# Attention and mixture of experts on one core: two more sets of prepared buffers, paid for by work in place

## The chip, the cores and the metric

The kernel runs on one core of one Trainium2 chip. The metric is the device time of one execution in microseconds. The core's engines work side by side, each through its own list of instructions in order: TensorE (PE, with PEld for its weight loads), VectorE (DVE), ScalarE (ACT), GpSimd (POOL) and SyncE (SP), which here only issues DMAs. An instruction that waits holds up everything behind it on its engine.

## The reference

Four batches of eight heads, 768 tokens, head size 40, run a recurrence with a decaying state; its output, laid out as 3072 tokens of 320 features, goes through a dense mixture of eight experts whose gate is balanced in eight rounds.

```python
for t in range(S):
    y[:, :, t] = np.einsum('bhd,bhde->bhe', rt, state)
    Sa = np.einsum('bhde,bhe->bhd', state, at)
    state = state * wt[:, :, None, :] - np.einsum('bhd,bhe->bhde', Sa, bt) + np.einsum('bhd,bhe->bhde', vt, kt)
...
P = np.exp(logits - logits.max())
for _ in range(8):
    P /= P.sum(1, keepdims=True) + 1e-09
    P /= P.sum(0, keepdims=True) + 1e-09
    P *= N / E
for e in range(E):
    out += P[:, e:e + 1] * (np.maximum(x @ w1[e], 0.0) @ w2[e])
```

## The kernel before

**Two phases.** `attention` runs the recurrence in chunks of 64 tokens: 12 chunks by 4 batches make 48 blocks, numbered 4c + b here. The mixture of experts follows and is the rest of the span. Its first eight blocks, like the whole attention phase, are put in order by a planner that simulates the engines' lists while the program is built; from its ninth block on (`N_MAN = 8`) the order is the one written.

**Preparing a block** is `prep(c, b)`. SyncE loads `inp` (112 rows of decays, k, b and a). VectorE scans the decays forward (`q`, L123), takes a reciprocal, and scans backward (`gf`, L133). SyncE stores `gf` to DRAM (`gd`, L137), from where the recurrence loads it as `gr`. GpSimd scales k and b (`kb`, L147) and a (`ab`, L153 and L154; VectorE does this for the first eight blocks). TensorE multiplies them (`ll`, L159). VectorE masks one half of the product into `sx` (L169), and ScalarE copies the other half, after `sx`, to `lt` (L173) and stores it to DRAM (`ld`, L178). What the recurrence needs later (`sx`, `bb`, `cc`) stays in one of `NSX = 20` sets, taken in turn. The first preparations use the last eight sets as scratch: `IN_SETS` for the load, `KB_SETS` for `kb` and `lt`. From block 8 on, `inp` is one of two buffers in turn; `gf` has two buffers of its own, and `lt` has one.

**Inverting.** The 48 blocks form six groups of eight. When all eight `ld` blocks of a group have landed, SyncE loads them into `lu` (L367) and VectorE inverts 128 triangular 32x32 matrices at once: seven pairs of product (L184) and sum (L187), then pairs L193 and L196 for the off-diagonal parts of size 8, 8 and 16. The part of size 16 is built with 2048 products at a time in `pr`. `finish` copies the inverse transposed (L356), and SyncE stores it twice (`ud`, `nd`). `tload` and `tmat` fetch it back for the two chunks of the group as `tt`.

**The recurrence** is `recur(c, b)`, in five steps spread over time. One block takes, among others, `f` (L269), `pm` (L289, which needs `tt`) and `ws` (L296) on VectorE, six groups of matmuls on TensorE, and `y` on GpSimd.

**Order.** The calls are sorted by a due time written by hand (`ev`), and the planner then fills each engine's list from them. Loads and stores all stand in SyncE's one list, except that `ld` from block 8 on is issued by ScalarE.

Of the kernel before, what the change touches and what calls it, by code (L numbers as in the profile page):

```python
# [11 lines left out]
F32 = mybir.dt.float32  # L12
# [17 lines left out]
def attention(ctx, tc, d, xd, ps, pq, pt, gs, lg):  # L30
    nc = tc.nc
# [6 lines left out]
    dr = ctx.enter_context(tc.tile_pool(name="a_dr", bufs=2, space=bass.MemoryType.DRAM))  # L38
    dr1 = ctx.enter_context(tc.tile_pool(name="a_dr1", bufs=1, space=bass.MemoryType.DRAM))

    cst = const.tile([128, 64 + 64 + 104 + 128 + 40 + 260], F32, name="cst")
    nc.sync.dma_start(out=cst, in_=d["cst"])
    mask_u = cst[0:64, 0:64]
    mask_f = cst[0:R2, 64:128]
    mask_p = cst[:, 128:232]
    ident = cst[:, 232:360]
    one65 = cst[0:RP, 400:660]
# [26 lines left out]
    c1_b = [const.tile([R2, NP, 104], F32, name=f"c1{i}") for i in range(2)]  # L74
    unf = inv.tile([128, 1056], F32, name="un")
    luf = inv.tile([128, 1056], F32, name="lu")
    prf = inv.tile([128, 2048], F32, name="pr")
    gtf = inv.tile([128, 256], F32, name="gt")
    un, lu, tn = (t[:, 0:1024].rearrange("u (a b) -> u a b", b=32) for t in (unf, luf, prf))
    und, lud = (t.rearrange("u (b x) -> u b x", x=264)[:, :, 0:256].rearrange("u b (c j) -> u b c j", j=32)  # L80
# [19 lines left out]
    def first_use(i):  # L100
        if i in fresh:
            fresh.discard(i)
            nc.gpsimd.memset(bb_b[i], 0.0)
            nc.scalar.copy(out=sx_b[i][64:128].rearrange("r p h x -> r (p h) x")[:, :, 64:104],
                           in_=cst[64:128, 360:400].unsqueeze(1).broadcast_to([64, 8, 40]))

    state = {"sx": 0, "ab": 0, "g1": 0, "vz": 0, "c1": 0, "tt": 0, "f": 0, "rb": 0, "x1": 0}

# [7 lines left out]
    def prep(c, b, ld):  # L116
        cb = c * NB + b
        inp = raws[IN_MAP[cb]][0:RP, 0:1029] if IN_MAP.get(cb) else pin.tile([RP, 1029], F32, name="inp", bufs=2)
        nc.sync.dma_start(out=inp, in_=d["inp"][c, b])
# [3 lines left out]
        nc.vector.tensor_tensor_scan(  # L123
            out=qf.rearrange("r p t -> r (p t)"), data0=inp[:, 0:260], data1=one65,
            initial=0.0, op0=ALU.mult, op1=ALU.add)
        q = qf[0:R2]
        g1 = rot("g1", g1_b)
        nc.vector.reciprocal(out=g1[:, :, 64], in_=qf[:, :, 64])
        sx = rot("sx", sx_b)
        i = next(j for j in range(NSX) if sx_b[j] is sx)  # L130
        bb, cc = bb_b[i], cc_b[i]
        gf = pin.tile([RP, NP, 65], F32, name="gf", bufs=2)
        nc.vector.tensor_tensor_scan(  # L133
            out=gf.rearrange("r p t -> r (p t)")[:, 259::-1], data0=inp[:, 260:0:-1],
            data1=g1.rearrange("r p t -> r (p t)")[:, 259::-1], initial=0.0, op0=ALU.mult, op1=ALU.add)
# [19 lines left out]
        nc.scalar.copy(out=sx[64:128, :, 0, 0:64], in_=ab[0:64, :, 0:64])
        nc.scalar.copy(out=sx[64:128, :, 1, 0:64], in_=ab[64:128, :, 64:128])
        ll = pq.tile([128, NP, 2, 64], F32, name="ll", tag="pq")
        for p in range(NP):
            nc.tensor.matmul(ll[:, p], lhsT=kb[:, p], rhs=ab[0:kb.shape[0], p], start=True, stop=True)  # L159
# [9 lines left out]
        nc.vector.tensor_tensor(  # L169
            out=sx[0:64, :, :, 0:64], in0=ll[0:64],  # L170
            in1=mask_u.unsqueeze(1).unsqueeze(1).broadcast_to([64, NP, 2, 64]), op=ALU.mult)
        if cb >= NKB:
            nc.scalar.activation(out=lt, in_=ll[64:128], func=AF.Copy, scale=-1.0)  # L173
        nc.scalar.copy(out=sx[0:64, :, :, 64:104], in_=kt[0:64, :, :, 0:40])
        nc.scalar.activation(out=bb[0:64, :, 0:40], in_=kt[64:128, :, 0, 0:40], func=AF.Copy, scale=-1.0)
        nc.scalar.activation(out=bb[64:128, :, 64:104], in_=kt[64:128, :, 1, 0:40], func=AF.Copy, scale=-1.0)
        if cb >= NKB:
            (nc.sync if cb < N_SP else nc.scalar).dma_start(out=ld[GRP[c][1], :, b], in_=lt)  # L178
        return dict(cc=cc, sx=sx, bb=bb)
# [15 lines left out]
            in1=m.unsqueeze(1).broadcast_to([nu, n_c, n_k, n_r]), op=ALU.mult)  # L195
        nc.vector.tensor_reduce(out=dst, in_=prv.rearrange("u c k r -> u c r k"), op=ALU.add, axis=AX.X)  # L196

    def inv_off(us, o, n, h):
        gt = gtf[us, 0:n * n].rearrange("u (c r) -> u c r", r=n)
        un_, lu_ = un[us], lu[us]  # L200
        if h == n:
            contract(us, gt, un_[:, o:o + n, o:o + n], lu_[:, o:o + n, o + n:o + 2 * n])
            contract(us, un_[:, o:o + n, o + n:o + 2 * n], gt, un_[:, o + n:o + 2 * n, o + n:o + 2 * n])
            return
        contract(us, gt[:, 0:h], un_[:, o:o + h, o:o + n], lu_[:, o:o + n, o + n:o + 2 * n])
        contract(us, gt[:, h:n], un_[:, o + h:o + n, o + h:o + n], lu_[:, o + h:o + n, o + n:o + 2 * n])
        contract(us, un_[:, o:o + n, o + n:o + n + h], gt[:, :, 0:h], un_[:, o + n:o + n + h, o + n:o + n + h])
        contract(us, un_[:, o:o + n, o + n + h:o + 2 * n], gt, un_[:, o + n:o + 2 * n, o + n + h:o + 2 * n])

    INV = [(inv_diag, (i,)) for i in range(1, 8)] + [(inv_off, a) for a in ((0, 8, 8), (16, 8, 8), (0, 16, 8))]  # L210
# [172 lines left out]
    for c in range(NCH):  # L383
# [3 lines left out]
        t = 5 * c + 2 - T_LEAD  # L387
# [67 lines left out]
def body(ctx, tc, d, out):  # L455
    nc = tc.nc
# [301 lines left out]
def _layout(inputs):  # L758
# [41 lines left out]
    cst[64:128, 64:128] = 1.0  # L800
    cst[0:64, 128:192] = up
    cst[64:128, 128:192] = up
    cst[:, 192:232] = 1.0
    cst[:, 232:360] = np.eye(128)
    cst[64:104, 360:400] = np.eye(40)
    cst[:, 400::65] = 1.0
# [20 lines left out]
```

## Time and profile before

| | |
|---|---|
| median of three runs | 1840.97 us (1838.9 to 1845.11) |
| profiled execution | 1844.61 us, its span 1842.7 us |
| granted TensorE clock, mean of the span | 0.961 |
| busy: PE, DVE, ACT, POOL | 94%, 75%, 46%, 47% |
| attention, to the last recurrence step | about 517 us |
| the six inverse copies (L356) start at | 95.23, 157.35, 234.02, 308.66, 382.89, 442.69 us |

The shares of busy time are means over two phases that differ. From 517 us on, in the mixture of experts, TensorE works nearly without a break. In the attention phase no engine is full, and what counts there is which wait ends last in each stage. The copies of the six inverses cut that phase into stages.

### The profile page before, as it was taken

The page shows a single profiled execution, that of the slowest core. Times are in us where ns is not written, and L with a number is a line of the kernel's source. Part 1 is how long each engine was busy: PE and PEld are TensorE (multiplying, and loading weights), DVE is VectorE, ACT ScalarE, POOL GpSimd, SP SyncE. Part 2 cuts the span into 40 slices and gives each one's busy share as a digit, 9 for nine tenths or more (in the row PEclk, how much of TensorE's full clock was granted, in tenths as well). Part 3 has the DMA queues.
Part 4 walks back from the last instruction along what each step waited for, and adds up shares of the span by engine and source line. Part 5 has one row for each costly group of instructions (what it writes and reads, how often), then busy time and mean ns, then how long its engine had stood idle before and what let it go on. Part 6 is the DMA issues. An engine that isn't in the chain of part 4 may idle for free.

```text
span 1842.7 us, 31504 instructions
## 1 busy us (share of the span) xinstructions
PE 1732.1 (94%) x11851; PEld 1697.6 (92%) x11851; DVE 1387.3 (75%) x2319; ACT 856.0 (46%) x1848; POOL 857.4 (47%) x844
## 2 busy tenths in 40 slices
PE   5488888899989999999999999999999999999999
PEld 4378888888889999999999999999999999999999
DVE  8876968877688768677776868977686877777676
ACT  6346667665643534344343433445343443425342
POOL 6545545532662617355371826007191744628170
PEclk8579899999899999999999999999999999999999
DMA  8467887875820102011110202201020111102001
GB/s 215 128 151 165 188 182 184 183 175 130 207 74 31 57 4 71 22 53 39 37 58 17 76 19 69 65 12 57 19 75 20 56 38 38 57 19 75 6 33 43
DMA packets 194957, 145.10 MB, mean 79 GB/s; under 512 B 143861, under 2 KB 171637, under 8 KB 194805
## 3 DMA queue, kind: packets, MB, share of 16 engines
q1 hardware_dynamic: 189013, 137.09, 28.7%
q10 hardware_dynamic: 5792, 6.00, 1.2%
q8 instruction: 94, 1.54, 0.3%
q14 instruction: 58, 0.48, 0.1%
HBM read 117.00 MB, written 26.04 MB: 78 GB/s over the span
## 4 chain that ended last, share of the span: by engine, by line
PE 73%; DVE 13%; DMA 7%; issue 3%; ACT 2%; POOL 1%; SPq 1%; ACTq 0%; DVEq 0%; POOLq 0%
PE op L636 36%; PE p L571 33%; DVE pr L193 2%; DVE un L196 2%; DMA inp<-in_inp_dram 2%; DVE gt L196 1%; DVE q L123 1%; DMA ld<-lt 1%; DMA lu<-ld 1%; DVE gf L133 1%; DMA td<-nd 1%; PE pu L287 1%; PE ll L159 1%; DMA rb<-in_r_dram 1%; DVE pm L289 1%
## 5 line engine op out<-in xcount | busy, mean ns | idle before, releaser
L571 PE MATMUL p<-xch,wh 128*128 128x384 f32 (+1 forms) x1792 | 604.8, 339 | 8.9 <-DVE sm L589 5.2
L592 ACT ACTIVATE hh<-sm 128x384 fp32r<-128x384 f32 x512 | 269.5, 527 | 725.3 <-DVE sm L589 725.3
L636 PE MATMUL op<-wh,hh 128*128 128x320 f32 x1536 | 476.8, 311 | 1.0 <-ACT hh L592 0.9
L636 PE MATMUL op<-wl,hh 128*128 128x320 f32 x1536 | 474.7, 310 | 0.0
L636 PE MATMUL op<-wh,hl 128*128 128x320 f32 x1536 | 467.3, 310 | 0.8 <-DVE hl L595 0.8
L517 POOL TENSOR_TENSOR wl<-ws,wh 128x640 fp32r<-128x640 f32 x60 | 103.0, 1716 | 608.3 <-ACT wh L515 608.2
L595 DVE SCALAR_TENSOR_TENSOR hl<-sm,hh 128x384 fp32r<-128x384 f32 x512 | 371.1, 758 | 2.4 <-ACT hh L592 2.0
L571 PEld LDWEIGHTS p<-xch,wh 128*128 128x128 f32 (+1 forms) x1792 | 337.2, 188 | 12.6 <-DVE sm L589 6.3
L571 PE MATMUL p<-xcl,wh 128*128 128x384 f32 x896 | 302.5, 338 | 0.0
L571 PE MATMUL p<-xch,wl 128*128 128x384 f32 x896 | 301.7, 337 | 0.0
L636 PEld LDWEIGHTS op<-wh,hh 128*128 128x128 f32 x1536 | 290.2, 189 | 1.6 <-ACT hh L592 1.5
L636 PEld LDWEIGHTS op<-wl,hh 128*128 128x128 f32 x1536 | 291.0, 189 | 0.0
L636 PEld LDWEIGHTS op<-wh,hl 128*128 128x128 f32 x1536 | 287.2, 188 | 1.1 <-DVE hl L595 1.0
L589 DVE TENSOR_TENSOR sm<-p,u 128x384 f32<-128x384 f32 x384 | 233.1, 617 | 8.8
L589 DVE TENSOR_TENSOR sm<-p,p 128x384 f32<-128x384 f32 x128 | 71.3, 557 | 129.8 <-PE p L571 76.3
L571 PEld LDWEIGHTS p<-xcl,wh 128*128 128x128 f32 x896 | 168.7, 188 | 0.0
L571 PEld LDWEIGHTS p<-xch,wl 128*128 128x128 f32 x896 | 168.6, 188 | 0.0
L589 DVE TENSOR_TENSOR p<-p,p 128x384 f32<-128x384 f32 x128 | 71.2, 556 | 102.6 <-PE p L571 102.2
L589 DVE TENSOR_TENSOR u<-p,p 128x384 f32<-128x384 f32 x128 | 70.9, 554 | 59.4 <-PE p L571 58.2
L525 POOL TENSOR_TENSOR wl<-ss,wh 128x512 fp32r<-128x512 f32 x60 | 89.7, 1496 | 28.3 <-ACT wh L522 24.2
L300 POOL TENSOR_TENSOR y<-ws,gr 104x256 f32<-104x256 f32 x48 | 47.1, 980 | 113.1 <-DVE ws L296 99.9
L700 DVE SCALAR_TENSOR_TENSOR acc<-op,pmat,acc 128x320 f32<-128x320 f32 x168 | 91.3, 544 | 4.5 <-PE op L636 4.4
(160 smaller groups left out, 2717.4 us busy)
## 6 DMA issues: line engine op xcount, KB each, us to landing
ws<-in_wts_dram SPq DMA_DIRECT2D x60, 832.0 KB
inp<-in_inp_dram SPq DMA_DIRECT2D x42, 450.2 KB
rb<-in_r_dram SPq DMA_DIRECT2D x48, 224.0 KB
gd<-gf SPq DMA_DIRECT2D x48, 113.8 KB
gr<-gd SPq DMA_DIRECT2D x48, 113.8 KB
vz<-in_v_dram SPq DMA_DIRECT2D x48, 112.0 KB
ld<-lt ACTq DMA_DIRECT2D x40, 128.0 KB
f<-in_vt_dram SPq DMA_DIRECT2D x48, 80.0 KB
```

What stands on the lines that cost most here:

```text
L123: nc.vector.tensor_tensor_scan(out=qf.rearrange("r p t -> r (p t)"), data0=inp[:, 0:260], data1=one65, initial=0.0, op0=ALU.mult, op1=ALU.add)
L193: nc.vector.tensor_tensor(out=prv, in0=a.unsqueeze(3).broadcast_to([nu, n_c, n_k, n_r]), in1=m.unsqueeze(1).broadcast_to([nu, n_c, n_k, n_ ...
L196: nc.vector.tensor_reduce(out=dst, in_=prv.rearrange("u c k r -> u c r k"), op=ALU.add, axis=AX.X)
L300: nc.gpsimd.tensor_tensor(out=y[:, :, b % 2], in0=ws[:, :, 0:64], in1=gr[0:R2, :, 64:0:-1], op=ALU.mult)
L517: g.tensor_tensor(out=wl[:, 0:640], in0=raw[:, 256:896], in1=wh[:, 0:640], op=ALU.subtract)
L525: g.tensor_tensor(out=lv[:, 3:7], in0=so[:, :, 0], in1=hv[:, 3:7, 0], op=ALU.subtract)
L571: nc.tensor.matmul(o, lhsT=w_, rhs=x_, start=(j == 0), stop=(j == 3))
L589: eng.tensor_tensor(out=out, in0=x, in1=y, op=ALU.add)
L592: nc.scalar.activation(out=hh[:, f, h], in_=sm[f][:, h], func=AF.Relu)
L595: v.scalar_tensor_tensor(out=hl[:, f, h], in0=sm[f][:, h], scalar=0.0, in1=hh[:, f, h], op0=ALU.max, op1=ALU.subtract)
L636: nc.tensor.matmul(ops[i], lhsT=a[:, h, cs], rhs=w_[:, cw], start=(f == 0 and h == 0 and j == 0), stop=(last and h == 1 and j == 2))
L700: nc.vector.scalar_tensor_tensor(out=acc[:, m], in0=ops[i], scalar=pmat[:, n, e:e + 1], in1=acc[:, m], op0=ALU.mult, op1=ALU.add)
```

## The change

The sets of prepared buffers become 22. The room comes from four places. The backward scan writes over the decays that it reads, in the load's buffer, so that `gf` has no buffer of its own, and `gd` is stored from there. From block 8 on, `lt` is written over the part of `inp` that held k and b, and `ld` is stored from there. The product tile `pr` shrinks from 2048 to 1024 elements, and the inverse's part of size 16 is built in six pieces that leave out rows and columns known to be zero, where four stood before. The table of constants loses its repeated parts. The gate's matrix, the ones and the identity of the second phase get their buffers after the attention phase has given up its own; the other buffers of the second phase stay where they were. The warm-up before the first inverse's end has seven matmuls of 296 columns instead of four of 512.

```diff
-    cst = const.tile([128, 64 + 64 + 104 + 128 + 40 + 260], F32, name="cst")
+    cst = const.tile([128, 64 + 104 + 128 + 260], F32, name="cst")
...
-    prf = inv.tile([128, 2048], F32, name="pr")
+    prf = inv.tile([128, 1024], F32, name="pr")
...
-        gf = pin.tile([RP, NP, 65], F32, name="gf", bufs=2)
+        gf = inp[:, 1:261].rearrange("r (p t) -> r p t", p=NP)
         nc.vector.tensor_tensor_scan(
-            out=gf.rearrange("r p t -> r (p t)")[:, 259::-1], data0=inp[:, 260:0:-1],
+            out=inp[:, 260:0:-1], data0=inp[:, 260:0:-1],
             data1=g1.rearrange("r p t -> r (p t)")[:, 259::-1], initial=0.0, op0=ALU.mult, op1=ALU.add)
         gd[c, b] = dr1.tile([RP, 260], F32, name=f"gd{cb}")
-        nc.sync.dma_start(out=gd[c, b], in_=gf.rearrange("r p t -> r (p t)"))
+        nc.sync.dma_start(out=gd[c, b], in_=inp[:, 1:261])
...
             kb = kb1
-            lt = pin.tile([64, NP, 2, 64], F32, name="lt")
+            lt = inp[0:64, 261:773].rearrange("r (p k t) -> r p k t", p=NP, k=2)
...
-    def inv_off(us, o, n, h):
+    def inv_off(us, o, n, rows):
...
+        m, e = o + n, o + 2 * n
+        for a, b in rows:
+            contract(us, gt[:, a:b], un_[:, o + a:o + b, o + a:m], lu_[:, o + a:m, m:e])
+        for a, b in [(n - y, n - x) for x, y in reversed(rows)]:
+            contract(us, un_[:, o:m, m + a:m + b], gt[:, :, 0:b], un_[:, m:m + b, m + a:m + b])
+
+    INV = [...] + [(inv_off, a) for a in ((0, 8, ((0, 8),)), (16, 8, ((0, 8),)), (0, 16, ((0, 4), (4, 8), (8, 16))))]
...
-        for _ in range(4):
-            nc.tensor.matmul(fl, lhsT=unf[:, 384:512], rhs=cst[:, 0:512], start=True, stop=True)
+        for _ in range(7):
+            nc.tensor.matmul(fl[:, 0:296], lhsT=unf[:, 384:512], rhs=cst[:, 0:296], start=True, stop=True)
...
-NSX = 20
+NSX = 22
...
-IN_SEQ = (19,18,17,16,0,0,19,18)
+IN_SEQ = (21, 20, 19, 18, 0, 0, 21, 20)
...
-        nc.gpsimd.memset(ones, 1.0)
-        nc.sync.dma_start(out=ident, in_=d["cst"][:, 232:360])
+    mid = ctx.enter_context(tc.tile_pool(name="mid", bufs=1))
...
+    nc.gpsimd.memset(ones, 1.0)
+    nc.sync.dma_start(out=ident, in_=d["cst"][:, 168:296])
```

The planner makes new lists from this, and three places of them matter here.

**SyncE behind the third inverse's copy, with the waits of each DMA.** Names with DMAHW are counters of DMAs that have landed, the others counters of an engine. Before, with the loads of the next group's `lu` ahead:

```order
L367 DMA lu<-ld 16x32x32 [waits DMAHW6_49,DMAHW2_49]
L367 DMA lu<-ld 16x32x32 [waits DMAHW7_49]
L367 DMA lu<-ld 16x32x32 [waits DMAHW0_49]
L367 DMA lu<-ld 16x32x32 [waits DMAHW1_49]
L257 DMA gr<-gd_965 112x260 [waits Pool_49]
L137 DMA gd_2660<-gf 112x260 [waits DMAHW3_49,DVE_49]
L119 DMA inp<-in_inp_dram 112x1029 [waits DMAHW4_49]
L255 DMA rb_212<-in_r_dram 112x512 [waits DMAHW5_49,PE_49]
L259 DMA f_209<-in_vt_dram 64x8x40 [waits DMAHW6_49]
L119 DMA inp<-in_inp_dram 112x1029 [waits DMAHW7_49,Pool_49]
```

Now, between the fetch of the inverse (`td`, `tt`) and the loads of `lu`, which come later:

```order
L222 DMA td<-nd 32x16x32 [waits DMAHW0_49]
L119 DMA inp<-in_inp_dram 112x1029 [waits DMAHW5_49,DMAHW1_49,Activation_49]
L224 DMA td<-ud 32x16x32 [waits DMAHW2_49]
L224 DMA td<-ud 32x16x32
L228 DMA tt_210<-ud 32x16x32 [waits DMAHW4_49]
L228 DMA tt_210<-ud 32x16x32
L228 DMA tt_210<-ud 32x16x32 [waits DMAHW6_49]
L228 DMA tt_210<-ud 32x16x32 [waits DMAHW7_49]
L301 DMA xd<-y 40x4x128 [waits DMAHW1_49]
L137 DMA gd_2334<-inp 112x260 [waits DMAHW2_49,DVE_49]
L301 DMA xd<-y 40x4x128 [waits DMAHW3_49]
L119 DMA inp<-in_inp_dram 112x1029 [waits DMAHW0_49,DMAHW4_49,Activation_49,Pool_49]
```

A load of `inp` used to wait for GpSimd, the last reader of the buffer's old contents, where it waited for an engine at all. It now waits for ScalarE, which writes `lt` into the buffer, and for the store of that `lt` to have landed. The two loads in the rows of before are those of blocks 33 and 34; block 32's stood three rows above them, and block 31's ahead of the inverse's stores. Those in the rows of now are blocks 31 and 32, so that block 31, the last of the group that `lu` waits for, is only loaded behind the inverse before it.

**VectorE ahead of the fourth inverse** (its first product is the row L184; the numbers behind `sx` are those of buffers). Before:

```order
L169 TENSOR_TENSOR sx_166<-ll,cst 64x8x64
L269 TENSOR_TENSOR f_209<-av,cst 104x8x64
L296 TENSOR_TENSOR ws<-c_2579,c_221 104x416
L289 TENSOR_TENSOR pm<-pu,cst 128x416
L123 SCALAR_TENSOR_TENSOR q<-inp,cst 112x260
L128 RECIPROCAL g_215<-q 112x4
L133 SCALAR_TENSOR_TENSOR gf<-inp,g_215 112x260
L269 TENSOR_TENSOR f_210<-av,cst 104x8x64
L184 TENSOR_TENSOR pr<-un,lu 128x4
```

Now:

```order
L123 SCALAR_TENSOR_TENSOR q<-inp,cst 112x260
L327 COPY lg<-lp 128x8
L128 RECIPROCAL g_224<-q 112x4
L133 SCALAR_TENSOR_TENSOR inp<-inp,g_224 112x260
L169 TENSOR_TENSOR sx_175<-ll,cst 64x8x64
L286 TENSOR_TENSOR pm<-pu,cst 128x416
L169 TENSOR_TENSOR sx_178<-ll,cst 64x8x64
L266 TENSOR_TENSOR f_217<-av,cst 104x8x64
L184 TENSOR_TENSOR pr<-un,lu 128x4
```

The last `sx` of the inverse's own group (block 31: `sx_166` before, `sx_175` now) stood four rows ahead of the scans of block 32; it now stands behind them.

**VectorE at the end of the first inverse** (the copy L356, now L353). Before:

```order
L169 TENSOR_TENSOR st_171<-ll,cst 64x8x64
L193 TENSOR_TENSOR pr<-gt,un 128x2048
L123 SCALAR_TENSOR_TENSOR q<-inp,cst 112x260
L196 TENSOR_REDUCE un<-pr 128x16x8
L128 RECIPROCAL g_215<-q 112x4
L169 TENSOR_TENSOR st_172<-ll,cst 64x8x64
L356 COPY pr<-un 128x1024
L133 SCALAR_TENSOR_TENSOR gf<-inp,g_215 112x260
L123 SCALAR_TENSOR_TENSOR q<-inp,cst 112x260
L128 RECIPROCAL g_215<-q 112x4
L133 SCALAR_TENSOR_TENSOR gf<-inp,g_215 112x260
L184 TENSOR_TENSOR pr<-un,lu 128x4
```

Now:

```order
L193 TENSOR_TENSOR pr<-gt,un 128x768
L133 SCALAR_TENSOR_TENSOR inp<-inp,g_224 112x260
L196 TENSOR_REDUCE un<-pr 128x16x4
L193 TENSOR_TENSOR pr<-gt,un 128x1024
L196 TENSOR_REDUCE un<-pr 128x16x4
L353 COPY pr<-un 128x1024
L169 TENSOR_TENSOR sx_187<-ll,cst 64x8x64
L123 SCALAR_TENSOR_TENSOR q<-inp,cst 112x260
L128 RECIPROCAL g_224<-q 112x4
L133 SCALAR_TENSOR_TENSOR inp<-inp,g_224 112x260
L169 TENSOR_TENSOR st_190<-ll,cst 64x8x64
L123 SCALAR_TENSOR_TENSOR q<-inp,cst 112x260
```

Before, 17 of the 48 scans `q` stood ahead of this copy, and four rows, with one more scan `q`, stood between the copy and the second inverse. Now 14 stand ahead, and three more preparations follow the copy before the second inverse. Up to the second copy there are `ws` of six blocks instead of four, and up to the last copy of 38 instead of 37.

More of the change, by code (lines that the diff above doesn't have):

```diff
@@ L39, in attention @@
     dr1 = ctx.enter_context(tc.tile_pool(name="a_dr1", bufs=1, space=bass.MemoryType.DRAM))
-    cst = const.tile([128, 64 + 64 + 104 + 128 + 40 + 260], F32, name="cst")
+    cst = const.tile([128, 64 + 104 + 128 + 260], F32, name="cst")
     nc.sync.dma_start(out=cst, in_=d["cst"])
     mask_u = cst[0:64, 0:64]
[L44 to L47, printed above, removed]
+    mask_f = cst[0:R2, 0:64]
+    mask_p = cst[:, 64:168]
+    ident = cst[:, 168:296]
+    one65 = cst[0:RP, 296:556]
     NTB = 2
@@ L104, in first_use @@
             nc.scalar.copy(out=sx_b[i][64:128].rearrange("r p h x -> r (p h) x")[:, :, 64:104],
-                           in_=cst[64:128, 360:400].unsqueeze(1).broadcast_to([64, 8, 40]))
+                           in_=ident[64:128, 64:104].unsqueeze(1).broadcast_to([64, 8, 40]))
     state = {"sx": 0, "ab": 0, "g1": 0, "vz": 0, "c1": 0, "tt": 0, "f": 0, "rb": 0, "x1": 0}
@@ L196, in contract @@
         nc.vector.tensor_reduce(out=dst, in_=prv.rearrange("u c k r -> u c r k"), op=ALU.add, axis=AX.X)
-    def inv_off(us, o, n, h):
+    def inv_off(us, o, n, rows):
         gt = gtf[us, 0:n * n].rearrange("u (c r) -> u c r", r=n)
         un_, lu_ = un[us], lu[us]
[L201 to L210, printed above, removed]
+        m, e = o + n, o + 2 * n
[3 more added lines that the diff above has]
+            contract(us, un_[:, o:m, m + a:m + b], gt[:, :, 0:b], un_[:, m:m + b, m + a:m + b])
+    INV = [(inv_diag, (i,)) for i in range(1, 8)] + [(inv_off, a) for a in ((0, 8, ((0, 8),)), (16, 8, ((0, 8),)), (0, 16, ((0, 4), (4, 8), (8, 16))))]
     def tload(c):
@@ L425 @@
 KB_POOL = (1,2,3,4,5,6,7)
-IN_SETS = (19, 18, 17, 16)
-KB_SETS = (15, 14, 13, 12)
-IN_SEQ = (19,18,17,16,0,0,19,18)
+IN_SETS = (21, 20, 19, 18)
+KB_SETS = (17, 16, 15, 14)
+IN_SEQ = (21, 20, 19, 18, 0, 0, 21, 20)
 IN_MAP = dict(enumerate(IN_SEQ))
@@ L461, in body @@
     one = ctx.enter_context(tc.tile_pool(name="one", bufs=1))
-    pmat = one.tile([128, 24, E], F32, name="pmat")
     lg = one.tile([128, 24, E], F32, name="lg")
-    ones = one.tile([128, 128], F32, name="ones")
-    ident = one.tile([128, 128], F32, name="ident")
     gs = one.tile([R2, NP, E], F32, name="gs")
@@ L472, in body @@
         attention(actx, tc, d, xd, ps, pq, pt, gs, lg)
-        nc.gpsimd.memset(ones, 1.0)
-        nc.sync.dma_start(out=ident, in_=d["cst"][:, 232:360])
+    mid = ctx.enter_context(tc.tile_pool(name="mid", bufs=1))
+    pmat = mid.tile([128, 24, E], F32, name="pmat")
+    ones = mid.tile([128, 128], F32, name="ones")
+    ident = mid.tile([128, 128], F32, name="ident")
+    nc.gpsimd.memset(ones, 1.0)
+    nc.sync.dma_start(out=ident, in_=d["cst"][:, 168:296])
     stg = ctx.enter_context(tc.tile_pool(name="stg", bufs=2))
@@ L794, in _layout @@
     gate[0:40], gate[64:104] = wg[0], wg[1]
-    cst = np.zeros((128, 660), np.float32)
+    cst = np.zeros((128, 556), np.float32)
     i = np.arange(64)
@@ L798, in _layout @@
     cst[0:64, 0:64] = up
+    cst[64:128, 0:64] = 1.0
     cst[0:64, 64:128] = up
[L800 to L806, printed above, removed]
+    cst[64:128, 64:128] = up
+    cst[:, 128:168] = 1.0
+    cst[:, 168:296] = np.eye(128)
+    cst[:, 296::65] = 1.0
     arrays = dict(inp=inp, r=rb.reshape(NCH, NB, RP, NP, 128), v=packed(g["v"]),
```

## The prediction

> **What bounds the kernel now.** I read the span and the busy time by stage first, then what VectorE waited for, then the order of time around one inverse. The page's span, and the stretches between the inverse copies (columns: stretch, length, then busy time of PE, PEld, DVE, ACT, POOL, granted clock, DMA share, GB/s):
>
> ```profile
> span 1842.7 us, 31504 instructions
> ```
>
> ```profile
> 95.20:157.00 61.80, 54.14 (x428) 47.48 (x427) 48.67 (x71) 33.91 (x85) 31.78 (x32) 0.82 0.71 158
> ...
> 234.00:308.60 74.60, 65.18 (x611) 61.18 (x610) 60.09 (x92) 50.81 (x129) 36.24 (x48) 0.93 0.81 183
> ...
> 442.80:517.00 74.20, 67.60 (x611) 64.47 (x610) 41.42 (x72) 47.55 (x108) 35.59 (x37) 0.91 0.71 175
> 517.00:1842.70 1325.70, 1311.11 (x8199) 1305.85 (x8197) 986.93 (x1702) 535.35 (x1055) 609.30 (x527) 1.00 0.13 43
> ```
>
> The last stretch, the mixture of experts, is full on PE (1311.1 of 1325.7), and the change leaves its work and nearly all of its order alone. So the time moves as the end of attention, about 517, moves. In a middle stage such as 234.00 to 308.60 neither PE (65.2) nor DVE (60.1) is full. What DVE waits for there:
>
> ```profile
> DVE q L123 <- DMA inp<-in_inp_dram: 5.6, 2, 2.8
> DVE sx L169 <- PE ll L159: 3.9, 2, 3.7
> ```
>
> These are waits of preparation. The stage is set by a loop: inverse ends, the last blocks of the next group are prepared, `ld` lands, `lu` is loaded, the next inverse runs. DVE in order of time, copies and first products of the inverses:
>
> ```profile
> 95.23 1.03 DVE L356 COPY pr<-un 128x1024 f32<-128x1024 f32 x1
> ...
> 105.94 0.17 DVE L184 TENSOR_TENSOR pr<-un,lu 128x4 f32<-128x4 f32 x1 [7.45 <-DMA td<-nd]
> ...
> 234.02 1.07 DVE L356 COPY pr<-un 128x1024 f32<-128x1024 f32 x1
> ...
> 257.75 0.17 DVE L184 TENSOR_TENSOR pr<-un,lu 128x4 f32<-128x4 f32 x1 [1.31 <-DMA lu<-ld]
> ...
> 442.69 1.06 DVE L356 COPY pr<-un 128x1024 f32<-128x1024 f32 x1
> ```
>
> From a copy's end to the next inverse's start pass 9.7 us behind the first copy (96.26 to 105.94), and 22.7 in the middle (235.09 to 257.75).
>
> **The change, part by part.** *The load's buffer is held longer: the largest cost.* Two buffers serve blocks 8 to 47. The load of block n+2 could start when block n's `ab` was made; now it waits until block n's `ld` has landed. In time order:
>
> ```profile
> 48.80 0.70 DVE L123 TENSOR_TENSOR_SCAN q<-inp,cst 112x260 f32<-112x260 f32 x1 [2.34 <-DMA inp<-in_inp_dram]
> ...
> 50.08 0.51 ACTq L178 DMA_DIRECT2D ld<-lt  x1
> ...
> 183.33 0.56 SPq L119 DMA_DIRECT2D inp<-in_inp_dram  x1
> ...
> 191.49 0.45 ACTq L178 DMA_DIRECT2D ld<-lt  x1
> ...
> 240.35 0.94 SPq L225 DMA_DIRECT2D td<-nd  x2
> ...
> 271.20 0.68 DVE L169 TENSOR_TENSOR st<-ll,cst 64x512 f32<-64x512 f32 x1
> ...
> 272.54 0.48 ACTq L178 DMA_DIRECT2D ld<-lt  x1
> ```
>
> Block 26's load went out at 183.33, block 24's `ld` at 191.49: 8.2 us of head start are gone, and the store's flight too. From `sx` (271.20) to the `ld` issue (272.54) pass 1.34. Stores and loads on the chain of waits, from issue to what they release:
>
> ```profile
> 44.40 4.31 DMA inp<-in_inp_dram
> ...
> 181.73 5.77 DMA inp<-in_inp_dram
> ...
> 247.77 5.01 DMA ld<-lt
> ...
> 256.59 5.25 DMA inp<-in_inp_dram
> ...
> 289.83 2.21 DMA ld<-lt
> ```
>
> A store takes 2.21 to 5.01, I take 3.6; a load 4.31 to 5.77, I take 5.0: the middles. From `sx` to the scan that may use the buffer again: 1.34 + 3.6 + 5.0 = 9.9 us (7.9 to 12.1). Durations of DVE's work between the first and the last copy (busy us and mean ns of one behind the bar):
>
> ```profile
> L269 DVE TENSOR_TENSOR f<-av,cst 104x512 f32<-104x512 f32 x38 | 25.7, 676 | 4.6 <-PE av L268 4.6
> L133 DVE TENSOR_TENSOR_SCAN gf<-inp,g 112x260 f32<-112x260 f32 x32 | 25.0, 780 | 0.2
> L123 DVE TENSOR_TENSOR_SCAN q<-inp,cst 112x260 f32<-112x260 f32 x31 | 22.8, 734 | 20.9 <-DMA inp<-in_inp_dram 20.9
> L289 DVE TENSOR_TENSOR pm<-pu,cst 128x416 f32<-128x416 f32 x38 | 22.0, 580 | 5.0 <-PE pu L287 5.0
> L296 DVE TENSOR_TENSOR ws<-c,c 104x416 f32<-104x416 f32 x37 | 21.4, 580 | 11.6 <-PE c L294 6.3 <-ACT lg L243 4.5 <-ACT sx L155 0.8
> ...
> L196 DVE TENSOR_REDUCE gt<-pr 128x128 f32<-128x2048 f32 x5 | 18.2, 3631 | 0.0
> L169 DVE TENSOR_TENSOR sx<-ll,cst 64x512 f32<-64x512 f32 x20 | 13.4, 672 | 8.8 <-PE ll L159 8.8
> L193 DVE TENSOR_TENSOR pr<-un,lu 128x2048 f32<-128x2048 f32 x5 | 12.2, 2450 | 0.0
> ...
> L196 DVE TENSOR_REDUCE gt<-pr 128x64 f32<-128x512 f32 x10 | 10.8, 1076 | 0.1
> ...
> L196 DVE TENSOR_REDUCE gt<-pr 128x128 f32<-128x1024 f32 x5 | 9.5, 1893 | 0.0
> ...
> L193 DVE TENSOR_TENSOR pr<-un,lu 128x512 f32<-128x512 f32 x10 | 6.8, 677 | 0.1
> L193 DVE TENSOR_TENSOR pr<-un,lu 128x1024 f32<-128x1024 f32 x5 | 6.5, 1302 | 0.0
> ...
> L128 DVE RECIPROCAL g<-q 112x4 f32<-112x4 f32 x31 | 5.3, 171 | 0.1
> ```
>
> *Inside an inverse* stand, by the new list, between the start of `sx` of block 33 and the scan of block 35: that `sx` and the next, a backward scan, three sums and two products of 512, a product of 1024, and `pm`, `f` and `ws` of the recurrence, 2 x 0.67 + 0.78 + 3 x 1.08 + 2 x 0.68 + 1.30 + 1.84 = 9.9 us of DVE work. That just covers the round of 9.9, so I keep the stage's waits as they are: 0, from -2.8 (the one wait of 2.8 inside an inverse goes) to three waits of 2.2 less 2.8, +3.8.
>
> *Between inverses* the new order is serial. Times from the copy's end: `td` is issued at 240.35 - 235.09 = 5.3 and its two issues take 0.9, so block 31's load starts at 6.2 and lands at 11.2. Its scans with the reciprocal between them (0.73 + 0.17 + 0.78 = 1.7) end at 12.9, and the `gd` issue ahead of block 32's load takes 0.4: 13.3. That load lands at 18.3, its scans end at 20.0, block 31's `sx` follows, its `ld` leaves at 21.3 and lands at 24.9. From `ld`'s landing to the inverse took 257.75 - 252.78 = 5.0: 29.9, against 22.7. So +7.2 (4.3 to 10.1). For one load instead of two it would be near zero.
>
> *The inverse.* Each half of the size-16 part makes 2816 products instead of 3072. Per 1024 a product costs 2.45 - 1.30 = 1.15 and a sum 3.63 - 1.89 = 1.74, and 0.15 each as a start. A half: -(1.15 + 1.74)/4 + 2 x 0.15 = -0.42, an inverse -0.85. A middle or the last stage: 7.2 + 0 - 0.85 = +6.4 (0.7 to 13.1), four of them +25.6. In two of them block n's load stands behind six more DMA issues, at 0.94/2 = 0.47 each: 2 x 2.8 = +5.6.
>
> *The first inverse.* Block 10's load (44.40) now waits for block 8's `ld` (50.08): its scan moves from 48.80 to 50.08 + 3.6 + 5.0 = 58.7. Against that and a like wait of block 12, three preparations fewer stand ahead of the copy, 3 x (0.73 + 0.78 + 0.67) = 6.5 of DVE work. I take +1 (0 to 4). *Behind it* those three come due, with much the same chain as above (block 15's and block 16's loads, then block 15's `sx`, 0.8 us earlier for one scan less): 29.1 us instead of 9.7. With two more steps of the recurrence in this stage, at 0.68 + 0.58 + 0.58 = 1.84 us of DVE each, and -0.85: 19.4 + 3.7 - 0.85 = +22.3 (19.5 to 29). *The tail*: 38 instead of 37 of the 48 steps are done at the last copy. The last step's `ws` on the chain:
>
> ```profile
> 516.34 0.60 DVE ws L296
> ```
>
> 516.94 - 443.75 for 11 steps is 6.7 each: -6.7.
>
> *The rest.* `gf` without a slot of its own saves a wait for `gd` that does not stand among DVE's longest: nothing. The scan in place has the same shape: nothing, unless overlap slows it. Two more first-use copies and clears on ACT and POOL, the ones, and a warm-up of 2072 columns for 2048 lie beside the early work. The late identity load stands in SP's list between loads of the recurrence and waits for the last preparation; covered, since preparation is over by then; if late it would hold the `vz` loads behind it.
>
> Sum: 1 + 22.3 + 25.6 + 5.6 - 6.7 = +47.8 on 1844.6, the profiled execution, which stands 3.6 above the median 1840.97: 1889. By the shortest transfers +22, by the longest +84.
>
> The Trainium skill, "SBUF — State Buffer", section "The DMA setup-cost knee", puts a DMA at 2 us plus its bytes at 436 GB/s: an estimate of 3.1 for this load and 2.3 for this store, whose sizes the page of the profile has:
>
> ```profile
> inp<-in_inp_dram SPq DMA_DIRECT2D x42, 450.2 KB
> ...
> ld<-lt ACTq DMA_DIRECT2D x40, 128.0 KB
> ```
>
> By it each gap would be 1.3 + 2 x 1.9 = 5.1 shorter and the one wait of 2.8 gone, and the sum 0 + 17.2 - 6.2 + 5.6 - 6.7 = +10. The trace agrees on the shortest store (2.21) and not on the loads (4.31 and up), with the DMA engines 0.81 busy. "DMA: Bandwidth & Descriptors", section "Rules for kernel authors", says to issue a DMA early and wait late; this change issues the loads later, and the rows above show the head start that it spends.
>
> **Rivals.** *The hold is covered (faster).* If `sx` to scan stays under 10 us and block 31's preparation does not lengthen the gap, only the gains are left: 6 x 0.85 = 5.1 and one step 6.7, 1829. It decides at a gap of 22.7, where store, two loads and `lu` must fit into 11 us. For it: the shortest rows, 2.21 and 4.31. Against: 3.6 + 10 + 5.0 = 18.6 by the middles. *PE covers it (no change).* PE is 65.2 of 74.6 busy; if the recurrence, now two steps ahead, set the end, a later inverse would cost nothing: 1841. Against: two steps are 2 x 6.7 = 13.4, less than the first stage's +22.3. *Waits add up (much slower).* Each late scan delays the next `sx`, that its `ld`, and that the load after the next; with the longest rows and such carry-over, +84 to +120: 1925 to 1960. For it: every load now also stands in SP's list behind others' waits.
>
> **How the numbers follow.** My forecast (+22 to +84, 1863 to 1925) 0.66; covered, faster 0.12; covered by PE 0.08; much slower 0.14. About 0.3% (5.5 us) can be told from no change. Slower 0.80, same 0.08, faster 0.12. The range 1836 to 1930 takes in the case of no change and the lower end of much slower, and leaves out the faster case and most of the last.
>
> **What would show it.** In the profile after: DVE's wait of `q` for `inp` well above 5.6 us a stage, SP's loads of `inp` waiting for `ld`, the second inverse starting near 126 rather than 105.94, the gaps at 28 us or more, the last copy near 497, and then ten steps at unchanged pace. Wrong if the gaps stay near 22 us, or if the copies come later and the end does not.

## The result, and the profile after

The changed kernel takes 1892.64 us (median of five runs, 1888.01 to 1895.92) against 1840.97: a ratio of 1.0274 with a 95% interval of 1.0251 to 1.0298, so it is slower by 51.7 us. Its profiled execution took 1895.92 us.

The same views as before, of the changed kernel. Its lines stand three lower: L353 is the inverse copy, L266 `f`, L364 the load of `lu`. The span, and the stretches between the inverse copies (stretch, length, busy time of PE, PEld, DVE, ACT, POOL, granted clock, DMA share, GB/s):

```profile
span 1894.1 us, 31554 instructions
```

```profile
87.70:169.90 82.20, 68.09 (x545) 62.97 (x546) 57.71 (x90) 45.23 (x114) 32.65 (x43) 0.83 0.69 147
...
259.70:343.50 83.80, 66.93 (x542) 63.08 (x541) 55.64 (x91) 44.47 (x113) 35.56 (x43) 0.80 0.66 148
...
567.70:1894.10 1326.40, 1311.48 (x8200) 1305.95 (x8198) 986.76 (x1702) 534.96 (x1055) 609.42 (x527) 1.00 0.13 43
```

The last stretch, the mixture of experts, is as long as before (1326.40 and 1325.70). All the time went into attention, whose last `ws` starts at 567.10 instead of 516.34:

```profile
567.10 0.59 DVE L293 TENSOR_TENSOR ws<-c,c 104x416 f32<-104x416 f32 x1 [0.24 <-PE c L291]
```

The first stage is 82.2 long instead of 61.8, at nearly the same granted clock (0.83 and 0.82). Over the whole of attention the clock is lower, 0.84 against 0.87, so it is a rival too. It does not account for the stretches between a copy's end and the next inverse's start, called gaps below: before, the third and the fourth gap were 22.7 and 22.0 us at a clock of 1.00 each; now they are 32.2 at 0.73 and 37.1 at 0.95, the longer one at the higher clock. What the lower clock adds elsewhere was not tested by itself.

What VectorE and SyncE waited for between 45 and 560 us (engine, line, releaser; then us in total, times, the longest):

```profile
DVE q L123 <- DMA inp<-in_inp_dram: 51.0, 21, 6.3
DVE sx L169 <- PE ll L159: 24.4, 9, 5.1
DVE pr L184 <- DMA lu<-ld: 13.9, 4, 6.0
```

```profile
SPq L119 <- DMA ld<-inp: 45.4, 24, 5.0
SPq L364 <- DMA ld<-inp: 8.3, 4, 5.0
```

In the same window of before no load of `inp` waited for an `ld`, and VectorE waited less for loads and for `ll`:

```profile
DVE q L123 <- DMA inp<-in_inp_dram: 23.4, 9, 5.2
...
DVE sx L169 <- PE ll L159: 11.0, 8, 3.7
```

Copies and first products of the inverses, in time order:

```profile
87.69 1.05 DVE L353 COPY pr<-un 128x1024 f32<-128x1024 f32 x1
...
119.07 0.17 DVE L184 TENSOR_TENSOR pr<-un,lu 128x4 f32<-128x4 f32 x1 [3.63 <-DMA lu<-ld]
...
343.47 1.04 DVE L353 COPY pr<-un 128x1024 f32<-128x1024 f32 x1
...
381.58 0.17 DVE L184 TENSOR_TENSOR pr<-un,lu 128x4 f32<-128x4 f32 x1 [6.02 <-DMA lu<-ld]
...
499.45 1.06 DVE L353 COPY pr<-un 128x1024 f32<-128x1024 f32 x1
```

Read so for all six inverses, the five gaps from a copy's end to the next first product were 9.7, 22.9, 22.7, 22.0 and 20.8 us before and are 30.3, 33.3, 32.2, 37.1 and 29.4 now: 98.0 and 162.3 in all. In these gaps VectorE stood idle for 107.3 us instead of 54.9. The first gap shows the round that the change brought (DVE, ACT's and SP's queues, in order of time):

```profile
88.66 0.67 DVE L169 TENSOR_TENSOR sx<-ll,cst 64x512 f32<-64x512 f32 x1
...
89.99 0.45 ACTq L178 DMA_DIRECT2D ld<-inp  x1
...
94.91 0.36 SPq L119 DMA_DIRECT2D inp<-in_inp_dram  x1
94.95 0.68 DVE L169 TENSOR_TENSOR st<-ll,cst 64x512 f32<-64x512 f32 x1 [3.05 <-PE ll L159]
99.79 0.48 ACTq L178 DMA_DIRECT2D ld<-inp  x1
99.80 0.70 DVE L123 TENSOR_TENSOR_SCAN q<-inp,cst 112x260 f32<-112x260 f32 x1 [4.17 <-DMA inp<-in_inp_dram]
...
104.04 0.36 SPq L119 DMA_DIRECT2D inp<-in_inp_dram  x1
108.72 0.70 DVE L123 TENSOR_TENSOR_SCAN q<-inp,cst 112x260 f32<-112x260 f32 x1 [6.25 <-DMA inp<-in_inp_dram]
```

`sx` at 88.66, its `ld` out at 89.99, the next load that may use this buffer at 94.91, its scan at 99.80: a round of 11.1. The next round, 94.95 to 108.72, takes 13.8, 4.8 of which pass between `sx` and the `ld` issue: ScalarE has written `lt` by 96.97, but two copies of `lg`, which wait for TensorE, stand ahead of the store in its list.

### The profile page after: what moved, and what is told of

The parts are those of the page before. It is cut to its first block, busy times and chain, and to the rows that moved or that the text cites. A ratio compares the mean times of both kernels' runs of the same rounds, so it can differ in the third digit from the quotient of the medians.

```text
span 1894.1 us, 31554 instructions
## 1 busy us (share of the span) xinstructions
PE 1753.6 (93%) x11857; PEld 1720.2 (91%) x11857; DVE 1390.5 (73%) x2343; ACT 855.9 (45%) x1850; POOL 850.5 (45%) x846
## 4 chain that ended last, share of the span: by engine, by line
PE 71%; DVE 4%; DMA 2%; issue 1%; POOL 0%; SPq 0%; ACT 0%; DVEq 0%; POOLq 0%; ACTq 0%
PE op L634 35%; PE p L569 33%; PE xc L273 1%; DVE pr L193 1%; PE pu L284 1%; DVE hl L593 0%; DVE gt L196 0%; DVE sm L587 0%; DVE un L196 0%; DMA ld<-inp 0%; PE c L291 0%; PE op L243 0%; DMA xd<-y 0%; PE lp L323 0%; PE av L265 0%
## 5 line engine op out<-in xcount | busy, mean ns | idle before, releaser
L159 PE MATMUL ll<-ab,kb 128*128 128x128 f32 x320 | 60.9, 350 | 51.4 <-POOL ab L154 45.0
L159 PEld LDWEIGHTS ll<-ab,kb 128*128 128x128 f32 x320 | 53.3, 252 | 56.0 <-POOL ab L154 48.1
L523 POOL TENSOR_TENSOR wl<-ss,wh 128x512 fp32r<-128x512 f32 x60 | 89.7, 1496 | 31.8 <-ACT wh L520 27.6
```

Of the source, the lines that this page charges most:

```text
L523: g.tensor_tensor(out=lv[:, 3:7], in0=so[:, :, 0], in1=hv[:, 3:7, 0], op=ALU.subtract)
```

## The experiments

Twelve kernels were run. Theory H: holding the load's buffer until the block's store has landed costs the time. Rivals: S, the 22 sets and the order laid for them; P, the scan in place is slower; I, the inverse in six pieces. The planner lays its lists anew for each kernel, so each differs in order too: the hold and the order that the planner lays for it are tested together, not apart. Ratios are to the kernel before on the same chip, with 95% intervals.

**Twenty sets.** From the changed kernel:

```diff
-NSX = 22
+NSX = 20
-IN_SETS = (21, 20, 19, 18)
+IN_SETS = (19, 18, 17, 16)
...
+    pad = padp.tile([128, 2512], F32, name="pad")
...
```

> The changed kernel with 20 sets instead of 22, the room of two sets left empty so that what follows keeps its addresses. Theory H (the load's buffer is held until the block's store has landed): the round trip store, load, scan stays in every stage, so the time stays above 1870 us (1870 to 1900), with the waits of q for inp near the 49.7 us of the changed kernel and gaps between inverses of 28 us or more. Rival S (22 sets and the order that the planner lays for them cost the time): back within 1836 to 1846 us, gaps 10 and 21 to 23 us. Rival P (the scan in place is slower) and rival I (the inverse in six pieces): stays near 1890, since both are still in it.

1890.94 us, 1.0273 (1.0252 to 1.0294), gaps 28.4, 35.6, 31.8, 37.9 and 29.1, copies within 2 us of the changed kernel's. S falls: under the hold two sets more are worth nothing, and cost nothing.

**A third load buffer.** From the changed kernel, paid for with one set:

```diff
-        inp = raws[IN_MAP[cb]][0:RP, 0:1029] if IN_MAP.get(cb) else pin.tile([RP, 1029], F32, name="inp", bufs=2)
+        inp = raws[IN_MAP[cb]][0:RP, 0:1029] if IN_MAP.get(cb) else pin.tile([RP, 1029], F32, name="inp", bufs=3)
...
-NSX = 22
+NSX = 21
...
```

> The changed kernel with a third load buffer, paid for with one set (21). Scan in place, store from the load's buffer and six pieces are kept. Theory H: the load of a block waits for the store three blocks earlier, about one block's work (10 us) more head start, which covers the 9.9 us round: 1836 to 1858 us, waits of q for inp near 20 us (changed kernel 49.7). Rivals P and I: nothing of theirs is taken away, 1880 us or more. Rival S: most of the sets are still there, 1865 or more.

1834.68 us, 0.9971 (0.9959 to 0.9984): the loss is gone, below the range that H gave. SyncE's waits, then VectorE's:

```profile
SPq L119 <- DMA ld<-inp: 35.5, 18, 4.7
```

```profile
DVE q L123 <- DMA inp<-in_inp_dram: 7.7, 10, 1.8
```

SyncE still waits 35.5 us for `ld`, but the scans behind those loads wait 7.7 us where they waited 51.0. P and I fall as causes, since both edits are still in this kernel.

**`lt` in the load's buffer, alone.** From the kernel before:

```diff
-            lt = pin.tile([64, NP, 2, 64], F32, name="lt")
+            lt = inp[0:64, 261:773].rearrange("r (p k t) -> r p k t", p=NP, k=2)
```

> The kernel before with one line changed: the block for the store (lt) is written into the load's buffer; the scan keeps its own buffer, 20 sets, the old inverse. Theory H: this alone brings the hold: 1865 to 1895 us, SP's loads of inp wait for ld, waits of q for inp 40 to 55 us (before 20.9). Rivals P, S and I: none of theirs is in it, 1836 to 1846 us.

1911.2 us, 1.0388 (1.036 to 1.0416). One line brings the whole loss and more; H's range was too low by 16 us. Its gaps sum to 170.2 us, 72 more than before, which is about the loss (70.5). The same two waits:

```profile
SPq L119 <- DMA ld<-inp: 52.8, 22, 5.8
```

```profile
DVE q L123 <- DMA inp<-in_inp_dram: 45.2, 20, 7.3
```

**The scan in place, alone.** From the kernel before:

```diff
-        gf = pin.tile([RP, NP, 65], F32, name="gf", bufs=2)
+        gf = inp[:, 1:261].rearrange("r (p t) -> r p t", p=NP)
...
-            out=gf.rearrange("r p t -> r (p t)")[:, 259::-1], data0=inp[:, 260:0:-1],
+            out=inp[:, 260:0:-1], data0=inp[:, 260:0:-1],
...
-        nc.sync.dma_start(out=gd[c, b], in_=gf.rearrange("r p t -> r (p t)"))
+        nc.sync.dma_start(out=gd[c, b], in_=inp[:, 1:261])
```

> The kernel before with the backward scan written over its own input and gd stored from there; lt keeps its own buffer, 20 sets, the old inverse. A load then waits for the store of gd instead of only for ab. Theory H: gd lands long before it is needed, 1838 to 1848 us, and the scans' mean tells alone what in place costs. Rival P (the scan in place is slower by 0.16 to 0.37 us a block, 48 blocks, as in the trace of the changed kernel, 926 against 764 ns in the mean): scans at 0.9 us or more and 1848 to 1860 us. Rivals S and I: 1836 to 1846 us.

1837.61 us, 0.9992 (0.9978 to 1.0006): no difference, 0.4 us below H's range and far below P's. The backward scans are longer, nearly as P said (0.89 us in the mean of all 48, where P had 0.9 or more). In the groups of the attention phase (busy us, mean ns), this run and then the kernel before:

```profile
L133 DVE TENSOR_TENSOR_SCAN inp<-inp,g 112x260 f32<-112x260 f32 x42 | 36.2, 862 | 0.4
...
L133 DVE TENSOR_TENSOR_SCAN st<-st,g 112x260 f32<-112x260 f32 x6 | 6.4, 1060 | 0.1
```

```profile
L133 DVE TENSOR_TENSOR_SCAN gf<-inp,g 112x260 f32<-112x260 f32 x42 | 32.1, 764 | 0.3
...
L133 DVE TENSOR_TENSOR_SCAN gf<-st,g 112x260 f32<-112x260 f32 x6 | 4.2, 692 | 0.6 <-DMA gd<-gf 0.6
```

The (862 - 764) x 42 + (1060 - 692) x 6 = 6.3 us do not show in the time.

**No product on GpSimd.** From the run just told, to see why the scans are longer:

```diff
-KB_POOL = (1,2,3,4,5,6,7)
+KB_POOL = ()
```

> The kernel before with the scan in place (1837.6 us) and the products kb of blocks 1 to 7 on VectorE instead of GpSimd. In the traces a backward scan takes 0.69 us alone and 1.1 to 1.7 where GpSimd multiplies kb at the same time. If the overlap is what lengthens a scan: the six scans in sets take 0.69 to 0.70 in the mean (1.06 with the products on GpSimd). If writing in place does: they stay at 1.06. The whole: 1836 to 1846 us.

```profile
L133 DVE TENSOR_TENSOR_SCAN st<-st,g 112x260 f32<-112x260 f32 x6 | 4.1, 688 | 0.0
```

688 ns, still in place. So in these six the overlap with GpSimd's product lengthens the scan, and writing in place does not. The other 42 keep their products on GpSimd and take 821 ns here. The whole took 1850.11 us, 1.0037 (1.0021 to 1.0053), above the expected range; why was not followed.

**The inverse, alone.** From the kernel before, `inv_off` and `pr` as in the changed kernel:

```diff
-    prf = inv.tile([128, 2048], F32, name="pr")
+    prf = inv.tile([128, 1024], F32, name="pr")
...
+    INV = [(inv_diag, (i,)) for i in range(1, 8)] + [(inv_off, a) for a in ((0, 8, ((0, 8),)), (16, 8, ((0, 8),)), (0, 16, ((0, 4), (4, 8), (8, 16))))]
...
```

> The kernel before with the inverse alone changed: the product tile halved, the large part in six pieces. By the groups of the trace of before a half of the large part falls by 0.42 us, six inverses by 5.1: 1833 to 1839 us if DVE's work inside an inverse lies on the path; within 1838 to 1844 if the stage's end is set by another wait. Theory H: no loss from it. Rival I: slower than 1846 us.

1836.19 us, 0.997 (0.995 to 0.9991): faster by 7.0 us, or 2 to 9. I falls. The pieces that stand for the 2048 products of one half (busy us, mean ns):

```profile
L193 DVE TENSOR_TENSOR pr<-un,lu 128x1024 f32<-128x1024 f32 x12 | 14.9, 1244 | 0.0
...
L196 DVE TENSOR_REDUCE gt<-pr 128x64 f32<-128x1024 f32 x6 | 11.3, 1884 | 0.1
...
L196 DVE TENSOR_REDUCE gt<-pr 128x64 f32<-128x768 f32 x6 | 8.6, 1434 | 0.0
...
L193 DVE TENSOR_TENSOR pr<-un,lu 128x768 f32<-128x768 f32 x6 | 5.6, 941 | 0.0
```

They make 1.24 + 1.88 + 1.43 + 0.94 = 5.50 us where the half took 3.63 + 2.45 = 6.08 in the rows of before: -0.58 here, where -0.42 was forecast. The other half went from 6.16 to 5.78 by its rows L193 and L196, -0.38. So the work saved is near the forecast, but the 7.0 us of the whole are another sum: in the profiled execution attention ends 13.7 us sooner than in the kernel before (503.2 against 516.9 us), and what follows it takes 5.3 longer (1331.1 against 1325.8), because the planner ordered the start of the mixture differently (see the better versions).

**Both edits of the buffer.** From the kernel before, `lt` in the load's buffer and the scan in place:

> The kernel before with lt written into the load's buffer and the scan in place as well, 20 sets, the old inverse. lt alone gave 1911 us, all of the changed kernel's edits with 20 sets 1891. Theory H with the scan's own buffers as a second link (a scan also waits for gd of the block two before): 1891 to 1899 us, the rest up to five for the six pieces. Rival: the inverse in six pieces made the difference of 20: 1905 to 1916 us.

1917.02 us, 1.04 (1.0384 to 1.0415), just above the rival's range and far above H's. The scan in place is no relief under the hold.

**With the six pieces added** to that:

> The kernel before with lt in the load's buffer, the scan in place and the inverse in six pieces: three of the changed kernel's edits, 20 sets, the rest of before. Without the six pieces it took 1917.0 us, all edits with 20 sets 1890.9. If the six pieces make the difference under the hold (the planner has more places to put preparations): 1885 to 1896 us, gaps near 33. If they save only what they saved alone (7.0 us): 1907 to 1913, and the rest of the edits (the constants, the late identity, the memory's layout) is worth the other 20.

1899.37 us, 1.0318 (1.0302 to 1.0334): between the two cases, 17.7 us less than without (15 by the ratios, since the two ran on different chips). In attention alone, by the profiled executions, the six pieces are worth 20.7 us under the hold (its end at 565.1 against 585.8) and 13.7 without it. The gaps sum to 160.0 against 188.3, while the time inside the inverses grows from 237.4 to 248.4: more preparation goes into the inverses (19 `sx` instead of 16). That the smaller pieces are what lets the planner put it there was not tested by itself. Of the remaining 8.4 us to 1890.9 the profiled executions show 4.8, and only 1.0 of them in attention, which ends at 565.1 and 564.1. So these three edits bring nearly the whole loss in attention.

**`lt` in its own tile.** From the changed kernel, with 21 sets:

```diff
-            lt = inp[0:64, 261:773].rearrange("r (p k t) -> r p k t", p=NP, k=2)
+            lt = pin.tile([64, NP, 2, 64], F32, name="lt")
...
-NSX = 22
+NSX = 21
...
```

> The changed kernel with a tile of its own for lt (paid for with one set, 21), two load buffers, scan in place, gd stored from the load's buffer, six pieces. Theory H: the hold until ld has landed is gone, only that until gd has landed is left: 1828 to 1842 us, waits of q for inp near 20 us. Rivals S and P: 1880 us or more.

1833.0 us, 0.9947 (0.9932 to 0.9962). With two buffers, the scan in place and the six pieces, the loss is gone once `ld` leaves from elsewhere, and the scans wait less than the 20 us that H gave. SyncE's and VectorE's waits:

```profile
SPq L119 <- DMA gd<-inp: 29.8, 21, 3.4
```

```profile
DVE q L123 <- DMA inp<-in_inp_dram: 9.1, 7, 2.5
```

The loads now wait for `gd`, which is stored some steps earlier than `ld`.

**Better versions.** All three have 20 sets and the six pieces: four load buffers with `lt` in them; three with `lt` in its own tile; three with `lt` and the scan's result each in their own tiles.

> The changed kernel with 20 sets and four load buffers, lt still in the load's buffer. Theory H: a third buffer brought the waits of q for inp from 51.0 to 7.7 us and the time to 1834.7; the fourth has little left to take: 1828 to 1837 us, waits under 8 us. If the three-buffer round still bound the stages, gaps would fall below 19 us and the time to 1825 or less.

> The version that the runs so far point to: 20 sets, three load buffers, lt in a tile of its own, scan in place, six pieces. Against 1833.0 us with 21 sets and two buffers: if loads are still late there (13.7 us of waits of q), 1825 to 1831; if the store through the recurrence and PE set the stages by now, 1830 to 1836, same as that one.

> As the run beside it, but the scan has its own two buffers again (as before). If the scan in place and its store hold anything up, this is 2 us or more faster than the run beside it; by theory H the two are the same within 4 us, 1828 to 1838.

| | us | ratio |
|---|---|---|
| four buffers | 1830.58 | 0.9943 (0.993 to 0.9957) |
| three, `lt` own | 1832.96 | 0.9957 (0.9944 to 0.997) |
| three, all own | 1827.01 | 0.9926 (0.9914 to 0.9939) |

The last one beats the kernel before by 15.1 us (1842.15 beside it). With four buffers the time is in H's range, and `q` waited 8.3 us for `inp`, just above H's 8 and no less than with three: the fourth buffer took nothing off these waits. With three and `lt` in its own tile it waited 2.2 us, and the time fell in the second case, in which other things set the stages. In the last one it waits 0.5 us for loads, and the longest waits of VectorE are those for the recurrence on TensorE:

```profile
DVE f L266 <- PE av L265: 30.7, 11, 6.6
DVE ws L293 <- PE c L291: 16.7, 15, 3.0
DVE q L123 <- POOL kb L147: 13.1, 9, 2.4
```

The 6 us between the last two are more than the 4 that H allowed. Neither the hold of the in-place store nor the scans' overlap shows as their cause: in the profiled executions, whose spans differ by 3.6 us, attention ends at 501.6 with `lt` alone in its own tile and at 502.6 with all, so the one with all is not ahead there. The difference lies behind attention, 1330.8 against 1326.2. At the start of the mixture TensorE waits for the gate's maximum in the first of the two, and in the last one it does not. Its waits from 501.64 to 561.64, with `lt` alone in its own tile:

```profile
PE mp L654 <- DVE sm L587: 3.7, 1, 3.7
PE p L569 <- DVE mxs L655: 2.5, 1, 2.5
```

In the last one the matmuls of the experts stand ahead of that for the maximum. The same two waits stand in the traces of the inverse alone and of the hold with six pieces, and neither in that of the kernel before. So a few microseconds between two of these kernels can come from how the planner ordered the start of the second phase, and not from the edit under test.

## Why the prediction was right, and where its terms were off

The mechanism was right, and the size came out at 51.7 us instead of 48. That the two are so close is partly luck: the first inverse came out 8.5 us below its term and the later gaps 9.3 above theirs, and the two errors cancel. Term by term, in the two profiled executions:

| term | forecast | measured |
|---|---|---|
| first inverse's copy | +1 | -7.5 |
| first gap | +19.4 | +20.7 |
| four later gaps, with the issues of DMAs | +34.4 | +43.7 |
| inside five inverses, with two more steps | -0.6 | -0.1 |
| tail | -6.7 | -6.0 |
| sum (47.8 there, by rounding) | +47.5 | +50.8 |

*First inverse: wrong.* Three preparations fewer stand ahead of the copy, as forecast (13 instead of 16 `sx`), which is worth 6.5 us, and the six pieces add 0.85. But the waits for held buffers that were to eat this up did not come. VectorE's wait up to the first copy, after and then before:

```profile
DVE q L123 <- DMA inp<-in_inp_dram: 1.3, 2, 0.8
```

```profile
DVE q L123 <- DMA inp<-in_inp_dram: 2.5, 2, 2.3
```

The step "its scan moves to 58.7" let VectorE stand idle until then. The scan came at 54.78, and VectorE did pieces of the first inverse in the meantime. So the second inverse started at 119.07 and not near 126.

*First gap: right by its own working.* Its steps were two loads one after the other, then `sx`, `ld` and `lu`, 29.1 us. The trace shows these two loads, the first of them 6.2 us behind the copy's end as forecast, and 30.3.

*Later gaps: too small by 9.3 in four.* Of this, 2.5 is the level before: 22.7 was taken for each, and they were 22.1 in the mean. Most of the rest lies in the step "block 31's load starts at 6.2", behind the issues of `td` (9.0 in the two stages with six more issues). The first loads of the four gaps leave 10.1, 6.8, 11.9 and 8.7 us behind the copy's end, 7.0 more in sum than forecast (the other steps of the chain cancel to within 0.2), and each waits for an `ld` last (1.4, 1.8, 1.8 and 2.2 us). That is the store of the block two before, whose `sx` in three of the four stands 3.3 to 4.8 us behind the copy. The prediction counted this hold inside the inverses and in the first one, and left it out at the start of a gap.

The round from `sx` to the scan was itself too small, taken as 9.9 us with bounds of 7.9 and 12.1. Over blocks 15 to 47 of the trace after it takes 11.6 in the mean, 9.0 to 16.4. Its parts: from `sx` to the `ld` issue 2.5 (1.34 was taken, one row, near the shortest of its kind: the mean over 40 blocks of before is 2.4), from there to the load's issue 4.2 (3.6 taken, for the flight alone; the load also stands in SyncE's list behind `gd` issues that wait for scans), from there to the scan 4.8 (5.0 taken).

*The last gap: near, by another way.* Behind the fifth copy only block 47's load is left. Of one load instead of two the prediction says that the lengthening "would be near zero", yet this gap grew by 8.6 us, from 20.8 to 29.4. In time order (SP's queue, then DVE):

```profile
441.25 0.33 SPq L119 DMA_DIRECT2D inp<-in_inp_dram  x1
...
445.75 0.70 DVE L123 TENSOR_TENSOR_SCAN q<-inp,cst 112x260 f32<-112x260 f32 x1 [4.54 <-DMA inp<-in_inp_dram]
...
451.98 0.68 DVE L169 TENSOR_TENSOR sx<-ll,cst 64x512 f32<-64x512 f32 x1 [3.60 <-PE ll L159]
```

From the scan to `sx` pass 6.2 us, in which GpSimd makes `kb` and `ab` and TensorE `ll`; for one load the prediction's chain has 1.7, the scans alone. In the four gaps with a second load this stretch is 9.5 to 10.0. By this comparison the second load adds about 3.5 us, and not the 7.1 of the chain.

*Inside the inverses: the sum is right.* It is 249.5 us before and 249.5 after, over five inverses, and the waits of `q` for loads there are 11.3 us against 10.2, so the rounds inside are nearly covered, as forecast. In the gaps these waits went from 10.6 to 38.4. The work inside is not the same, though: 17 `sx` instead of 24 and `ws` of 32 blocks instead of 25.

*The rest.* The last recurrence steps keep their pace (67.2 us for ten, 6.7 each). The six pieces save inside the five inverses what was forecast, in the run with them alone (244.5 us against 249.5, where 5 x 0.85 = 4.3 was forecast). That the whole moved by 7.0, near the 5.1, is luck: it is the sum of the 13.7 and 5.3 above. "The scan in place: nothing, unless overlap slows it" holds for the time; the scans did get longer, by 6.3 us of VectorE's time where the scan in place stands alone, with no loss of time. The two extra sets are worth nothing under the hold.

*The rivals.* "The hold is covered" needed gaps of 22.7. That is what a third buffer makes of it: gaps of 10.8, 16.2, 20.2, 19.8 and 20.5. "PE covers it" fell with the end of attention at 567. "Waits add up" did not come: with the large inverse pieces kept the hold took 1911 and 1917 us, above the changed kernel but still below this rival's 1925.

The estimate by the Trainium skill, "SBUF — State Buffer", section "The DMA setup-cost knee", gave +10; the trace does not agree. The shortest of the 33 rounds come near its 2.3 for the store and 3.1 for the load (2.3 and 3.6), the means of 4.2, SyncE's list included, and 4.8 do not, with other transfers in flight and the DMA share at 0.66 and 0.69 in the two stages shown.

## What to carry to other kernels

Before a buffer is reused for a block's output, count what it is held for: not only until its last reader, but until the store has landed, and then the next load's flight on top. With two buffers this whole round must fit under the work of one other block; a third buffer, or a small tile of its own for the output, took the loss away here. The price was one or two sets, and two sets were worth nothing in the one comparison made, under the hold. A transfer's price is the mean from what releases it to what it releases, queue included (4.2 and 4.8 us here), and not the shortest row (2.3 and 3.6). The first load behind a long piece of work deserves a look of its own: ask which store it waits for, and where that store's data is made.

## What the runs showed of the hardware that was not expected

A backward scan takes 0.69 us alone and up to 1.7 when GpSimd's product `kb` has started just before it. In other places the product is the longer one. In time order, after, two pairs and a scan alone:

```profile
304.56 1.88 POOL L147 TENSOR_TENSOR kb<-inp,q 104x512 f32<-104x512 f32 x1 [0.89 <-PE kt L167]
304.77 0.68 DVE L133 TENSOR_TENSOR_SCAN inp<-inp,g 112x260 f32<-112x260 f32 x1
...
361.34 1.18 POOL L147 TENSOR_TENSOR kb<-inp,q 104x512 f32<-104x512 f32 x1 [7.67 <-DVE q L123]
361.51 1.56 DVE L133 TENSOR_TENSOR_SCAN inp<-inp,g 112x260 f32<-112x260 f32 x1
...
369.36 0.70 DVE L133 TENSOR_TENSOR_SCAN inp<-inp,g 112x260 f32<-112x260 f32 x1
```

The profile's spans on GpSimd are rough, but the difference is large. In the second pair the product keeps its 1.18 us, and the scan ends at 363.07, 0.55 after the product's end. In the first pair the scan keeps 0.68, and the product takes 1.88, 0.70 more. In each of these pairs one of the two pays. The kernel before has such scans too (1.62 us at 179.73, 254.24 and 328.16), and there its own `gf` buffers were in use, so it is no matter of writing in place.

The Trainium skill, "SBUF — State Buffer", section "Who interferes with whom", says that a VectorE instruction with two inputs in SBUF contends with a GpSimd instruction that reads SBUF, and that the order of issue decides which one is blocked. In the two pairs shown the trace agrees that one side alone is held: the product for 0.70 us, about the scan's length, and the scan for 0.88, less than the product's 1.18. What decides which one can't be read here: in both pairs the product's record begins first.
